# Splitting a weight load to start the first FFN products on four banks, with packed query transposes and re-placed exponentials and loads

## Chip, cores, metric

The kernel runs on one core of one Trainium2 chip. The metric is the device time of a whole execution in microseconds (us). The profile is one execution, with times from the start of the core's span. A load has *landed* when the trace records the last of its completions. (The prediction and the expectations speak of last packets and of instruction fetches instead, on a clock that reads about 0.24 us more than the timelines shown here: the fetch put at 17.35 us there starts at 17.11 us here.)

## The reference, cut to what matters

```python
# 8 batches, 8 heads, 1024 rows, head size 64, 64 projected rows
k_proj = einsum('ks,bhsd->bhkd', E, k);  v_proj = einsum('ks,bhsd->bhkd', F, v)
attn = softmax(q @ k_proj^T / sqrt(64));  x = attn @ v_proj       # then (8192, 512)
h = maximum(maximum(x @ w1, x @ w2), x @ w3)                       # 512 -> 768
out = h @ w_out                                                    # 768 -> 512
```

## The kernel before

All engines are scheduled by hand: program order is execution order on each engine. Batch by batch, the FFN of one batch runs on TensorE (PE) while the attention of the next is slipped between its products. PE writes into eight PSUM banks. `two()` and `bank()` deal them out at build time by an estimated clock.

At the start, the loads are queued in the order of need. The first FFN products, half-batch 0 of batch 0, take six banks and begin once the first two quarters of w1 are there:

```python
    load_w(0, slice(0, 2))          # w1, quarters 0 and 1
    load_kv(2, V2); load_kv(2, V3)  # v of head pairs 2 and 3
    load_w(0, slice(2, 3)) ...
    # before the first product, while waiting for w1:
    v_pair(1); idle(1); x(1); z(2); z(3); at(18.2)

    def up_first(work):             # (cut) products of w1, quarter by quarter
        h = [... for t, ns in (two(), two(), two()) for n in (0, 1)]
        for ct in range(NCT):
            for jt in jts:
                up_mm(h[jt][0], 0, 0, 0, jt, (ct,))
                then((0, ct, jt))   # attention pieces hung behind a product
```

`v_pair(g)` projects v of head pair g (PE, then a VectorE copy), `z(g)` are the softmax sums, `x(g)` the values times the inverse sums. `qp` turns q of the second half-batch on PE, `sc` are scores (PE) with their exp (ScalarE), `za` sums, inverse and values together. `plan(b)` says behind which FFN step of batch b each piece of batch b+1 runs:

```python
        if b == 0: ...
                (1, 2): [vproj(1), ld(2)],
                (1, (3, "mid")): [sc(1, 0), sc(1, 1)],
                (1, 4): [za(1, 0), sc(1, 2)],
        if b == 1: ...
                (0, 3): [kproj(2), vproj(2), ld(3, (0, 1))],     # q and k of batch 3
                (0, 8): [zc(2, nc.gpsimd), ld(3, (2,))],         # broadcasts; v of batch 3
```

`zc(2)` computes batch 2's inverse sums compactly, writes them to DRAM (`zd`) and broadcasts them back into `zi_all` by four DMAs.

The softmax here doesn't subtract the row's maximum and nothing guards it: scores larger than these inputs give would overflow.

## Time and profile before

| reading | value | view |
|---|---|---|
| time, median of 3 | 403.15 us (403.04 to 403.41) | timing |
| span, PE busy, granted clock | 401.0 us, 97%, 1.00 | the page |
| chain that ended last | 80% PE, 11% DMA | the page |
| PE waits that matter | 1.3 us for w1; 0.3 for batch 1's v; 0.7 for hT | waits |

From the page, the busy times and the shares of the chain that ended last, kernel before:

```profile
PE 388.7 (97%) x2261; PEld 176.7 (44%) x2303; DVE 203.3 (51%) x319; ACT 149.0 (37%) x238; POOL 34.1 (9%) x48
PE 80%; DMA 11%; DVE 3%; issue 2%; ACT 2%; POOL 1%; DVEq 0%; ACTq 0%; POOLq 0%
```

The waits of PE in the kernel before (who waited for whom: total us, times, longest):

```profile
PE banks L567 <- DMA w_sb<-in_moe_w_dram: 1.3, 1, 1.3
...
PE banks L664 <- DVE hT L577: 0.7, 1, 0.7
PE banks L470 <- DMA k_t<-in_k_dram: 0.6, 1, 0.6
...
PE banks L345 <- DMA v_t<-in_v_dram: 0.3, 1, 0.3
```

PE is full, so time can only be gained by taking away its waits (5.5 us in all in the list of waits, without 1.6 us that end in "issue", for which the trace names no cause) or its work. The timeline says where these waits are. A line is: start, duration, engine, source line, operation, output<-input, count, and in brackets the idle time before it and what ended that.

PE in the kernel before, timeline:

```profile
16.63 0.62 PE L496 MATMUL banks<-v_t,efT 128*128 128x128 bf16 x8
17.08 0.38 PE L441 MATMUL banks<-warm 128*128 128x512 bf16 x1
...
19.44 1.24 PE L567 MATMUL banks<-xT,w_sb 128*128 128x512 bf16 x5 [1.29 <-DMA w_sb<-in_moe_w_dram]
...
38.75 0.48 PE L211 MATMUL banks<-qT,kpT 64*64 64x256 bf16 x4
...
55.95 1.06 PE L345 MATMUL banks<-v_t,efT 128*64 128x256 bf16 x16 [0.32 <-DMA v_t<-in_v_dram]
...
66.78 0.41 PE L231 MATMUL banks<-pT,ones 64*64 64x512 bf16 x4 [0.35 <-DVE xT L308]
...
67.21 0.57 PE L211 MATMUL banks<-qT,kpT 64*64 64x512 bf16 x4
...
117.83 0.39 PE L664 MATMUL banks<-wout_sb,hT 128*128 128x512 bf16 x1 [0.70 <-DVE hT L577]
```

The line at 16.63 is `v_pair(1)`; its start will be the mark from which stretches are counted. The wait at 117.83 begins with a DMA: the broadcasts of batch 2's inverse sums are issued late, and VectorE's scaling waits for them. GpSimd in the kernel before, timeline:

```profile
104.81 2.58 POOL L275 DMA_DIRECT2D zi_all<-zd  x4 [15.42 <-DMA zd<-zic]
```

VectorE in the kernel before, timeline:

```profile
112.63 2.35 DVE L308 TENSOR_TENSOR xT<-banks,zi_all 128x1024 bf16<-128x1024 f32 x2 [1.70 <-PE banks L567]
```

The bracket names PE, but PE's values were done at 110.8 us. The trace records the second broadcast as landed at 112.50 us, just before the scaling starts: that is the wait. The broadcasts were late because the store of `zd`, issued at 99.76 us, landed only at 104.27, at nearly the same time as batch 3's k (104.52), which was queued before it.

### The profile page before, as it was taken

To read this page: it belongs to the slowest core of one execution; us is meant where nothing else is said; L and a number is where in the kernel's file an instruction comes from. 1 tells how busy PE (TensorE), PEld (TensorE's weight loads), DVE (VectorE), ACT (ScalarE), POOL (GpSimd) and SP (SyncE) were. 2 spreads that over 40 slices of the span, in tenths; PEclk is the share of its full clock that TensorE was granted. 3 is DMA by queue.
4 is the path that set the end of the run, shared out by engine and by line. 5 is a ranking of instruction groups with operands and counts; after the bars stand their busy time and mean duration, and the time that the engine had idled before them with its cause. 6 is when DMAs were issued, how large, how long until landed. Compare 5 with 4: busy or idle time off the path is not lost.

```text
span 401.0 us, 5737 instructions
## 1 busy us (share of the span) xinstructions
PE 388.7 (97%) x2261; PEld 176.7 (44%) x2303; DVE 203.3 (51%) x319; ACT 149.0 (37%) x238; POOL 34.1 (9%) x48
## 2 busy tenths in 40 slices
PE   7899999999999999999999999999999999999996
PEld 3444444353435435444454445444454444444443
DVE  3348755761673525826274544744267342745251
ACT  2622537527213452253323542245323533132312
POOL 7340002010301000200020000200000000000000
PEclk9999999999999999999999999999999999999999
DMA  9999999969799989999899959992890229020202
GB/s 157 206 205 207 231 202 156 240 137 187 222 183 253 191 171 209 174 227 181 205 222 180 236 122 217 211 235 63 203 217 2 105 65 252 3 106 0 105 2 105
DMA packets 66315, 66.11 MB, mean 165 GB/s; under 512 B 30608, under 2 KB 58768, under 8 KB 66288
## 3 DMA queue, kind: packets, MB, share of 16 engines
q0 software_dynamic: 29088, 30.41, 47.2%
q1 hardware_dynamic: 37056, 35.20, 34.9%
q8 instruction: 18, 0.29, 0.3%
q10 hardware_dynamic: 144, 0.13, 0.1%
q14 instruction: 9, 0.07, 0.1%
HBM read 69.73 MB, written 16.97 MB: 216 GB/s over the span
## 4 chain that ended last, share of the span: by engine, by line
PE 80%; DMA 11%; DVE 3%; issue 2%; ACT 2%; POOL 1%; DVEq 0%; ACTq 0%; POOLq 0%
PE banks L567 54%; PE banks L664 18%; DMA v_t<-in_v_dram 8%; DMA w_sb<-in_moe_w_dram 3%; PE banks L345 3%; PE banks L231 2%; DVE xT L308 2%; PE banks L211 2%; PE banks L256 1%; ACT zi_all L297 1%; ACT zl L291 1%; DVE m L629 1%; DVE hT L577 0%; POOL k_t L152 0%; POOL q_t L157 0%
## 5 line engine op out<-in xcount | busy, mean ns | idle before, releaser
L567 PE MATMUL banks<-xT,w_sb 128*128 128x512 bf16 x1119 | 254.8, 379 | 3.8 <-DMA w_sb<-in_moe_w_dram 1.3
L567 PEld LDWEIGHTS <-w_sb 128*128 128x128 bf16 x1152 | 110.0, 98 | 137.5 <-issue 8.7
L629 DVE TENSOR_TENSOR m<-banks,h1s 128x512 f32<-128x512 f32 x90 | 62.1, 690 | 135.7 <-ACT h1s L625 92.4
L625 ACT COPY h1s<-banks 128x512 f32<-128x512 f32 x90 | 52.6, 585 | 119.7 <-PE banks L567 119.6
L664 PE MATMUL banks<-wout_sb,hT 128*128 128x512 bf16 x370 | 85.8, 379 | 1.7 <-issue 0.8
L577 DVE TENSOR_TENSOR hT<-banks,m 128x512 bf16<-128x512 f32 x90 | 62.3, 692 | 10.4 <-PE banks L567 0.8
L664 PEld LDWEIGHTS <-hT 128*128 128x128 bf16 x378 | 35.3, 98 | 48.8 <-issue 5.8
L102 ACT COPY o_sb<-banks 128x512 f32<-128x512 f32 (+1 forms) x56 | 32.6, 582 | 58.7 <-PE banks L664 58.3
L222 ACT ACTIVATE pT<-banks 128x1024 bf16<-128x1024 f32 (+1 forms) x36 | 32.7, 932 | 25.3 <-PE banks L211 25.3
L308 DVE TENSOR_TENSOR xT<-banks,zi_all 128x1024 bf16<-128x1024 f32 x28 | 33.2, 1220 | 12.0 <-PE banks L231 5.5
L200 POOL DMA_DIRECT2D q_t<-in_q_dram x7 | 6.1, 877 | 192.9 <-DMA qT<-q_p 102.4
L102 DVE CAST vp<-banks 64x256 bf16<-64x256 f32 (+1 forms) x18 | 7.1, 397 | 12.4 <-ACT vp L102 8.8
L345 PEld LDWEIGHTS <-efT 128*64 128x64 bf16 x224 | 11.6, 110 | 3.8 <-issue 3.0
L102 ACT CAST vp<-banks 64x256 bf16<-64x256 f32 x14 | 5.1, 364 | 20.7 <-PE banks L345 20.6
L231 PE MATMUL banks<-pT,vp 64*64 64x512 bf16 (+1 forms) x144 | 11.4, 363 | 0.4 <-DVE vp L102 0.4
L211 PE MATMUL banks<-qT,kpT 64*64 64x512 bf16 (+1 forms) x144 | 11.2, 361 | 0.0
L291 ACT ACTIVATE zl<-banks 128x512 f32<-128x512 f32 (+1 forms) x12 | 8.9, 739 | 5.2 <-PE banks L231 4.4
L102 DVE COPY q_p<-q_t 128x1024 bf16<-128x1024 bf16 x28 | 10.1, 425 | 0.0
L102 DVE COPY o_sb<-banks 128x512 f32<-128x512 f32 (+1 forms) x9 | 5.8, 654 | 4.5 <-PE banks L644 4.5
L441 PE MATMUL banks<-warm_f 128*128 128x512 f32 x8 | 6.6, 977 | 1.5 <-DVE warm_f L175 1.5
L345 PE MATMUL banks<-v_t,efT 128*64 128x256 bf16 x112 | 7.3, 273 | 0.3 <-DMA v_t<-in_v_dram 0.3
L345 PE MATMUL banks<-k_t,efT 128*64 128x256 bf16 x112 | 7.5, 276 | 0.0
(60 smaller groups left out, 119.0 us busy)
## 6 DMA issues: line engine op xcount, KB each, us to landing
out_dram<-o_sb SPq DMA_DIRECT2D x30, 512.0 KB, 5.0
zi_all<-zd SPq DMA_DIRECT2D x20, 512.0 KB, 7.9
q_t<-in_q_dram POOLq DMA_DIRECT2D x7, 1024.0 KB, 9.5
k_t<-in_k_dram POOLq DMA_DIRECT2D x7, 1024.0 KB, 16.0
v_t<-in_v_dram POOLq DMA_DIRECT2D x7, 1024.0 KB, 21.1
zi_all<-zd POOLq DMA_DIRECT2D x4, 512.0 KB, 8.0
w_sb<-in_moe_w_dram POOLq DMA_DIRECT2D x5, 384.0 KB, 12.6
k_t<-in_k_dram POOLq DMA_DIRECT2D x2, 512.0 KB, 8.8
```

Source lines behind the costliest of these rows:

```text
L102: done = {"v": nc.vector.tensor_copy, "s": nc.scalar.copy, "g": nc.gpsimd.tensor_copy}[eng](out=o, in_=i)
L211: nc.tensor.matmul(out=t[c * HALF:(c + 1) * HALF, hp, 0:n * P], lhsT=kpTs[b][rows, g, :], rhs=qTs[b][rows, at:at + n, :], start=True, stop ...
L222: nc.scalar.activation(out=pTs[b, g, lo], in_=t, func=AF.Exp, scale=scale)
L231: nc.tensor.matmul(out=t[hp * HALF:(hp + 1) * HALF, c, 0:nsi * HALF], lhsT=w(rows, hp), rhs=p[rows, hp, :], start=True, stop=True,)
L291: nc.scalar.activation(out=zl, in_=t, func=AF.Ln)
L308: nc.vector.tensor_tensor(out=xTs[b][:, g, lo:lo + nsi, :].rearrange("a (c s) p -> a c (s p)", c=2), in0=t, in1=zi, op=ALU.mult,)
L345: nc.tensor.matmul(out=t[hh * HALF:(hh + 1) * HALF, 0:width], lhsT=efT[:, si, (kv - 1) * KP:kv * KP], rhs=qkv[b][kv][:, heads[hh], si, :], ...
L567: nc.tensor.matmul(out=h, lhsT=w_sb[i][:, ct, jt * P:(jt + 1) * P], rhs=xTs[b][:, ct, ch * SPC:(ch + 1) * SPC, :], start=(ct == first), st ...
L577: nc.vector.tensor_tensor(out=o, in0=h, in1=other, op=ALU.max)
L625: nc.scalar.copy(out=h1s, in_=h[0][0])
L629: nc.vector.tensor_tensor(out=m12, in0=h[1][0], in1=h1s, op=ALU.max)
L664: nc.tensor.matmul(out=o_ps, lhsT=hTs[b, ch][:, jt, tt * P:(tt + 1) * P], rhs=wout_sb[:, jt, :], start=(jt == 0), stop=(jt == NJT - 1),)
```

## The change

The intent is to start the first FFN products as soon as one quarter of w1 is there, on four banks, with the rest of the attention start between them; to turn the second half of q as full-width packed transposes; and to re-place some exps and loads of the later schedule. The diff, cut:

```diff
-    load_w(0, slice(0, 2))
+    load_w(0, slice(0, 1))
+    load_w(0, slice(1, 2))
...
+    def pack_q(b, gs, lo, nsi):        # VectorE copies two heads side by side
...
     def qp(b, gs, lo, nsi):
-                heads_q(b, g, range(lo, lo + nsi), t[:, i * n:(i + 1) * n])
+                for si in range(nsi):
+                    nc.tensor.transpose(... in_=q_pk[b][:, g, lo + si] ..., identity=ident)
...
     v_pair(1)
-    idle(1)
-    x(1)
-    z(2)
-    z(3)
-    at(18.2)
+    at(17.4)
...
-        for ct in range(NCT):
-            for jt in jts:
+        for ct, js in (
+            (0, range(0, 4)), (1, range(0, 4)), (0, range(4, 6)), (1, range(4, 6)),
+            (2, jts), (3, jts),
+        ):
+            for jt in js:               # banks taken two at a time, when first needed
...
-                (1, (3, "mid")): [sc(1, 0), sc(1, 1)],
-                (1, 4): [za(1, 0), sc(1, 2)],
+                (1, (3, "mid")): [sc(1, 0, now=True), sc(1, 1)],
+                (1, 4): [za(1, 0), sc(1, 2, now=True)],
...
-                (0, 3): [kproj(2), vproj(2), ld(3, (0, 1))],
+                (0, 3): [kproj(2), vproj(2), ld(3, (0,))],
-                (0, 8): [zc(2, nc.gpsimd), ld(3, (2,))],
+                (0, 8): [zc(2, nc.gpsimd), ld(3, (1, 2))],
...
-                (1, 6): [vx(3, 2), vx(3, 3), sc(4, 0)],
+                (1, 7): [vx(3, 2), vx(3, 3), sc(4, 0)],
...
+                    (0, 0, 1): [lambda: x(1)],
+                    (0, 0, 3): [lambda: z(2), lambda: z(3)],
+                    (0, 1, 3): [lambda: v_pair(2), lambda: x(2)],
...
-                    (2, "a", 2): [qp(0, (0, 1), *c1)],
-                    (2, "a", 4): [qp(0, (2, 3), *c1)],
-                    (2, 0): [sc(0, 0, *c1)],
-                    (2, 2): [sc(0, 1, *c1)],
+                    (2, "a", 0): [pack_q(0, (0, 1), *c1)],
+                    (2, "a", 1): [pack_q(0, (2, 3), *c1)],
+                    (2, "a", 4): [qp(0, (0, 1), *c1)],
+                    (2, "a", 5): [qp(0, (2, 3), *c1)],
+                    (2, 1): [sc(0, 0, *c1)],
+                    (2, 3): [sc(0, 1, *c1)],
```

More of the change, by code (lines that the diff above doesn't have):

```diff
@@ L361, in heads_q, with qp, f @@
         pe(0.08 * len(sis))
-    def qp(b, gs, lo=0, nsi=SI):
+    q_pk = {}
+    def pack_q(b, gs, lo, nsi):
         def f():
-            if b not in qTs:
-                qTs[b] = att.tile([P, NPAIR * SI, P], BF16, name="qT")
+            if b not in q_pk:
+                q_pk[b] = att.tile([P, NPAIR, SI, 2, D], BF16, name="q_p", bufs=1)
+            for g in gs:
+                copy(
+                    "v", q_pk[b][:, g, lo:lo + nsi].rearrange("p si h d -> p h si d"),
+                    qkv[b][0][:, 2 * g:2 * g + 2, lo:lo + nsi], (), 0.25,
+                )
+        return f
+    def qp(b, gs, lo, nsi):
+        def f():
             t, ns = two()
@@ L370, in f @@
             for i, g in enumerate(gs):
-                heads_q(b, g, range(lo, lo + nsi), t[:, i * n:(i + 1) * n])
+                for si in range(nsi):
+                    nc.tensor.transpose(
+                        out=t[:, i * n + si * P:i * n + (si + 1) * P],
+                        in_=q_pk[b][:, g, lo + si].rearrange("p h d -> p (h d)"),
+                        identity=ident,
+                    )
+                pe(0.06 * nsi)
             o = qTs[b].rearrange("a (g si) p -> a g si p", si=SI)
@@ L590, in up_first @@
         jts = range(NJT)
-        h = [(t[:, n], ns[n:n + 1]) for t, ns in (two(), two(), two()) for n in (0, 1)]
-        for ct in range(NCT):
-            for jt in jts:
+        h = {}
+        for ct, js in (
[3 more added lines that the diff above has]
+            for jt in js:
+                if jt not in h:
+                    t, ns = two()
+                    for n in (0, 1):
+                        h[jt + n] = t[:, n], ns[n:n + 1]
                 up_mm(h[jt][0], 0, 0, 0, jt, (ct,))
@@ L753 @@
                 up_first({
-                    (0, 0, 5): [lambda: v_pair(2)],
-                    (0, 1, 2): [lambda: x(2)],
+                    (0, 0, 1): [lambda: x(1)],
+                    (0, 0, 3): [lambda: z(2), lambda: z(3)],
+                    (0, 1, 3): [lambda: v_pair(2), lambda: x(2)],
                     (0, 1, 5): [lambda: v_pair(3), ld(1)],
-                    (0, 2, 2): [lambda: x(3)],
-                    (2, "a", 2): [qp(0, (0, 1), *c1)],
-                    (2, "a", 4): [qp(0, (2, 3), *c1)],
-                    (2, 0): [sc(0, 0, *c1)],
-                    (2, 2): [sc(0, 1, *c1)],
+                    (0, 2, 1): [lambda: x(3)],
+                    (2, "a", 0): [pack_q(0, (0, 1), *c1)],
[4 more added lines that the diff above has]
+                    (2, 3): [sc(0, 1, *c1)],
                     (2, 4): [za(0, 0, *c1, then=True), sc(0, 2, *c1)],
```

## The prediction

> **What bounds the kernel now.** TensorE: the page shows PE busy 97% of 401.0 us at a granted clock of 1.00, and 80% of the chain of waits is PE. Three of its waits matter. (a) Until 19.2 us for w1's first part (1.3 us; first product at 19.44). (b) At 55.5 us the value projection of batch 1 waits for v (PE 0.3, weight loads 0.8 us); the DMA engines are full from 3 to 59 us, and v's last packet ends at 55.9. (c) At 117.8 us a down product waits 0.70 us for hT.
>
> **What the change does.**
> 1. *Split of w1's first part, start on four banks.* Half of it should land 0.95 us earlier (the whole took 1.9 us per DMA engine), and gains more: the packet records show one engine about 1 us late because a 16,384-byte instruction fetch sat on it from 17.35 to 18.33 us (the Trainium skill, "Runtime: NRT & Kernel Launch", Instruction fetch mechanics, says streams are refilled in 16 KiB blocks by DMA; this trace agrees, 18 such packets). The first half should pass before the fetch: landed at 17.4, first product at 17.6 us, 1.8 us earlier. The second half still lands near 19.2. But x(1) and the sums of pairs 2 and 3 (0.7 us on PE, done before while waiting) now follow the start, and x(2) directly follows its v_pair, a stall of about 0.5 us (copy 0.29 plus handovers). Net at the first pass's last part (25.16 before): 0.4 to 0.8 us earlier.
> 2. *Packed q.* 32 half-width transposes (0.64 us per 16) become 16 full-width (0.77 for 8 in the E/F turn): no gain on PE. Four more DVE copies, about 0.25 us each (1024 wide took 0.42), behind maxima that end at 33.4: up to 0.3 us of stall.
> 3. *Then PE meets (b).* Batch 1's v is limited by the bytes queued since the start: near 55.9 us again; the wait grows by what the start won. So 1 and 2 count as about 0.
> 4. *Exps of batch 1 at once:* may remove waits at 66.4 and 76.3 us (0.35 and 0.16), may add bank waits: 0.1 gained.
> 5. *k of batch 3 later, behind the zi broadcasts.* Before, k's load ran to 104.4 us, the zi issue waited until 104.8, and DVE's first batch-2 scaling stood until 112.6 (1.7 us idle) for the broadcast; the maxima behind it made (c). Now the broadcasts start about 2 us earlier and (c) should go: 0.7 gained. The price: v of batch 3 comes near 127.5 to 128.5 instead of 124.2, and is wanted at about 128: 0.2 lost on average, perhaps 1.
> 6. *Batch 2, step (1,7):* 0 to 0.2 gained.
>
> **Sum:** -0.7: **402.5 us, range 401.4 to 403.5.** Faster by over 2%: 0.01; within 2%: 0.98; slower: 0.01.
>
> **What would show it.** Timeline: first FFN product near 17.6, last part of the first pass near 24.6, PE's wait for batch 1's v 0.8 to 1.3 us, that projection at 55.6 to 56.3 as before. PE waits: no 0.7 us on hT near 117; DVE's first batch-2 scaling near 111. A PE wait on v near 127 would show step 5's price.
>
> **What would make it wrong.** If batch 1's v lands earlier too, the start's 0.5 us stays: 402.0 or less. If the packed copies or the changed bank order stall PE by a microsecond, or batch 3's v is over 1 us late: equal or worse.

## The result, and the profile after

The changed kernel takes 403.22 us (median of 4, 402.96 to 403.75), the kernel before 403.10 in the same rounds. The ratio is 1.0005, 95% interval 0.9987 to 1.0022: the same. (A ratio here is the mean time of one kernel's fast runs over that of the other's in the same rounds, so not quite the ratio of the quoted medians.) All outputs are right. In a second call it was 402.40 against 402.78, ratio 0.9988 (0.9966 to 1.0009): again the same.

From the page, kernel after:

```profile
PE 392.7 (98%) x2286; PEld 176.6 (44%) x2286; DVE 204.1 (51%) x323; ACT 149.0 (37%) x238; POOL 34.4 (9%) x49
PE 84%; DMA 8%; DVE 3%; ACT 2%; issue 2%; POOL 1%; DVEq 0%; POOLq 0%; ACTq 0%
```

PE's busy time rose by 4.0 us in a span of equal length. This is not more work: the profile before lacks records, showing 1119 products with w_sb where it has 1152 weight loads for them, and the one after shows all 1152. The changed kernel profiled once more (e11) shows 1119 again, and 387.8 us busy. The Trainium skill, "Trainium Kernel Development and Optimization", Performance Expectations, calls matmul busy time a bad metric for how close a kernel is to roofline, because matmuls are pipelined. Busy time misleads, but for another reason, missing records; no run here tests the reason that the skill gives.

The waits of PE, kernel after:

```profile
PE banks L346 <- DMA v_t<-in_v_dram: 0.7, 1, 0.7
PE banks L232 <- DVE vp L102: 0.7, 2, 0.5
PE banks L212 <- ACT zl L292: 0.5, 1, 0.5
PE banks L490 <- DMA k_t<-in_k_dram: 0.5, 1, 0.5
PE banks L386 <- DVE qT L102: 0.3, 1, 0.3
...
PE banks L212 <- DVE m L652: 0.3, 1, 0.3
```

Both aims were reached: the waits for w1 and for hT are gone. In their place stand waits for copies, for a logarithm of ScalarE, for a maximum of VectorE, and for a v. PE, kernel after, timeline:

```profile
16.53 0.62 PE L516 MATMUL banks<-v_t,efT 128*128 128x128 bf16 x8
17.32 0.59 PE L583 MATMUL banks<-xT,w_sb 128*128 128x512 bf16 x2 [0.17 <-DVE xT L309]
...
34.66 0.61 PE L386 MATMUL banks<-ident,q_p 128*128 128x128 bf16 x8 [0.35 <-DVE qT L102]
...
39.08 0.30 PE L212 MATMUL banks<-qT,kpT 64*64 64x256 bf16 x4 [0.52 <-ACT zl L292]
...
55.72 1.06 PE L346 MATMUL banks<-v_t,efT 128*64 128x256 bf16 x16
...
66.20 0.41 PE L232 MATMUL banks<-pT,ones 64*64 64x512 bf16 x4
...
66.76 0.37 PE L212 MATMUL banks<-qT,kpT 64*64 64x512 bf16 x1
67.40 0.41 PE L212 MATMUL banks<-qT,kpT 64*64 64x512 bf16 x3 [0.27 <-DVE m L652]
...
128.80 1.06 PE L346 MATMUL banks<-v_t,efT 128*64 128x256 bf16 x16 [0.71 <-DMA v_t<-in_v_dram]
```

The first product comes at 17.32 instead of 19.44 us. The score at 39.08 is the one that stood at 38.75 before without a wait. The line at 128.80 is batch 3's value projection and says 0.71; that v belongs to batch 3, not to batch 1. GpSimd and then VectorE, kernel after, timeline (the second a fence of its own):

```profile
102.18 2.38 POOL L276 DMA_DIRECT2D zi_all<-zd  x4 [12.86 <-DMA zd<-zic]
```

```profile
110.89 2.35 DVE L309 TENSOR_TENSOR xT<-banks,zi_all 128x1024 bf16<-128x1024 f32 x2
```

The store of `zd`, issued at 99.80 us, now landed at 101.61, the broadcasts went out 2.6 us earlier, and VectorE's scaling followed its own work without a wait.

To see who gave and who took, I cut PE's timeline at points that all versions have, and take differences of start times. The **mark** is the start of `v_pair(1)`. A mark is needed because the first loads do not land at the same time in each execution: over the 14 profiles (kernel before, changed kernel, 12 experiments) the first key projection started between 9.58 and 10.92 us, whatever the kernel. That spread alone is larger than most effects below. It also makes repeated runs scatter: 11 runs of the kernel before went from 401.85 to 404.91.

| stretch on PE, us | before | after | after, second profile |
|---|---|---|---|
| mark to first FFN product | 2.81 | 0.79 | 0.78 |
| A: mark to FFN of half-batch 1 | 29.85 | 30.11 | 29.99 |
| B: to batch 1's value projection | 9.47 | 9.08 | 9.07 |
| C: to batch 2's key projection | 29.05 | 29.32 | 29.31 |
| D: to batch 3's key projection | 42.87 | 41.99 | 41.99 |
| E: to batch 3's value projection | 0.90 | 1.77 | 0.90 |
| F: to the last down products | 267.44 | 267.47 | 267.44 |
| mark to last, sum of A to F | 379.58 | 379.74 | 378.70 |

The start is 2.0 us earlier (first row), and nothing of it is left at the end of A. About three quarters is gone within the first pass of products, as foreseen: its last part starts at 24.64 us, against 25.16 before, since `x(1)`, `z(2)` and `z(3)`, which ran inside the wait for w1 before, now follow the start, and PE waits 0.45 us for the copy behind `v_pair(2)`. The last half microsecond is what e5 and e7 look for. C loses 0.27, D gains 0.88, and E took 0.87 back in the first profile and nothing in the second. Two thirds of the run, F, did not notice anything.

### The profile page after: what moved, and what is told of

Same layout as the page of the kernel before. It is cut to its first block, busy times and chain, and to the rows that moved or that the text cites. A ratio compares the mean times of both kernels' runs of the same rounds, so it can differ in the third digit from the quotient of the medians.

```text
span 401.0 us, 5752 instructions
## 1 busy us (share of the span) xinstructions
PE 392.7 (98%) x2286; PEld 176.6 (44%) x2286; DVE 204.1 (51%) x323; ACT 149.0 (37%) x238; POOL 34.4 (9%) x49
## 4 chain that ended last, share of the span: by engine, by line
PE 84%; DMA 8%; DVE 3%; ACT 2%; issue 2%; POOL 1%; DVEq 0%; POOLq 0%; ACTq 0%
PE banks L583 55%; PE banks L687 18%; DMA v_t<-in_v_dram 6%; PE banks L346 3%; PE banks L232 2%; PE banks L212 2%; DMA k_t<-in_k_dram 2%; DVE xT L309 1%; PE banks L257 1%; ACT zl L292 1%; DVE hT L593 1%; ACT zi_all L298 1%; PE banks L490 1%; DVE m L652 0%; PE banks L461 0%
## 5 line engine op out<-in xcount | busy, mean ns | idle before, releaser
L583 PE MATMUL banks<-xT,w_sb 128*128 128x512 bf16 x1152 | 257.6, 379 | 0.3 <-DVE xT L309 0.3
L687 PE MATMUL banks<-wout_sb,hT 128*128 128x512 bf16 x378 | 86.9, 380 | 0.1
L102 DVE COPY q_p<-q_t 128x1024 bf16<-128x1024 bf16 (+1 forms) x32 | 11.3, 417 | 0.0
```

What stands on the lines that cost most here:

```text
L102: done = {"v": nc.vector.tensor_copy, "s": nc.scalar.copy, "g": nc.gpsimd.tensor_copy}[eng](out=o, in_=i)
L583: nc.tensor.matmul(out=h, lhsT=w_sb[i][:, ct, jt * P:(jt + 1) * P], rhs=xTs[b][:, ct, ch * SPC:(ch + 1) * SPC, :], start=(ct == first), st ...
L687: nc.tensor.matmul(out=o_ps, lhsT=hTs[b, ch][:, jt, tt * P:(tt + 1) * P], rhs=wout_sb[:, jt, :], start=(jt == 0), stop=(jt == NJT - 1),)
```

## Experiments

Theory: leads are swallowed one by one by waits whose end does not depend on PE's lead, either DMAs or another engine's queue. Rivals: the later schedule loses what the start gains; the packed turns cost the lead; the exps and not the load order took the hT wait away. Every run was timed in 5 rounds beside the kernel before.

| run | median, us | before, us | ratio to before (95%) |
|---|---|---|---|
| e1_start_only | 403.66 | 402.58 | 1.0017 (1.0000 to 1.0034) |
| e2_plan_only | 402.09 | 402.58 | 0.9981 (0.9965 to 0.9996) |
| e3_k_half_early | 402.62 | 402.58 | 0.9993 (0.9978 to 1.0007) |
| e4_one_w1_part | 403.81 | 402.58 | 1.0034 (1.0007 to 1.0060) |
| e5_score_later | 402.57 | 402.76 | 0.9992 (0.9976 to 1.0008) |
| e6_score_later_k_half | 402.66 | 402.76 | 0.9993 (0.9979 to 1.0007) |
| e7_old_q_turn | 402.40 | 402.76 | 0.9990 (0.9977 to 1.0004) |
| e8_old_load_order | 403.50 | 402.76 | 1.0014 (0.9999 to 1.0029) |
| e9_best | 402.18 | 402.78 | 0.9980 (0.9960 to 1.0001) |
| e10_best_v_later | 401.56 | 402.78 | 0.9966 (0.9944 to 0.9988) |
| e11_changed_again | 402.40 | 402.78 | 0.9988 (0.9966 to 1.0009) |
| e12_old_start | 401.47 | 403.25 | 0.9956 (0.9943 to 0.9970) |

The stretches of the same runs, in the letters of the table above:

| run | first product | A | B | C | D | E |
|---|---|---|---|---|---|---|
| e1_start_only | 0.79 | 29.99 | 9.27 | 29.05 | 42.88 | 0.90 |
| e2_plan_only | 2.94 | 29.98 | 9.36 | 29.31 | 41.99 | 0.90 |
| e3_k_half_early | 0.79 | 29.99 | 9.07 | 29.31 | 41.99 | 0.90 |
| e4_one_w1_part | 1.42 | 30.64 | 9.07 | 29.31 | 42.00 | 0.90 |
| e5_score_later | 0.79 | 29.56 | 9.51 | 29.31 | 42.00 | 0.89 |
| e6_score_later_k_half | 0.78 | 29.81 | 9.10 | 29.31 | 42.00 | 0.89 |
| e7_old_q_turn | 0.78 | 29.29 | 9.33 | 29.31 | 42.00 | 0.89 |
| e8_old_load_order | 0.79 | 29.99 | 9.19 | 29.31 | 42.48 | 0.90 |
| e9_best | 0.78 | 29.35 | 10.36 | 29.05 | 42.00 | 0.89 |
| e10_best_v_later | 0.79 | 29.32 | B+C 38.74 | | 42.00 | 0.90 |
| e12_old_start | 1.46 | 29.42 | B+C 38.14 | | 41.99 | 0.90 |

Where B+C is given, batch 1's value projection was moved; before, B+C is 38.52. F was 267.43 to 267.47 in all of them. C and D repeat to 0.01 us among profiles of the same code, so they are a far finer ruler than the times. A is less good: e5 and e6, with the same code there, differ by 0.25 us, because in e6 the v of pair 2 landed later. B depends on when the loads of that execution came: over the 14 profiles batch 1's v landed between 55.10 and 56.57 us, while the mark moved from 16.48 to 17.81 us, and the two do not move together. An execution with a late mark therefore waits less in B, and its end counted from the mark looks better than it is.

### One half of the change each: e1 and e2

e1 is the changed kernel with the `plan` of before; e2 is the kernel before with the `plan` of the changed one.

```diff
 e1 (against the changed kernel), e2 the other way round (against the kernel before)
-                (1, (3, "mid")): [sc(1, 0, now=True), sc(1, 1)],
-                (1, 4): [za(1, 0), sc(1, 2, now=True)],
+                (1, (3, "mid")): [sc(1, 0), sc(1, 1)],
+                (1, 4): [za(1, 0), sc(1, 2)],
-                (0, 3): [... ld(3, (0,))],      (0, 8): [... ld(3, (1, 2))],
+                (0, 3): [... ld(3, (0, 1))],    (0, 8): [... ld(3, (2,))],
-                (1, 7): [vx(3, 2), vx(3, 3), sc(4, 0)],
+                (1, 6): [vx(3, 2), vx(3, 3), sc(4, 0)],
```

> Only the start of the change (split of w1's first part, four banks, packed q); the later schedule as before. Theory (leads are swallowed one by one): first FFN product near 17.3 us and about 0.5 us of lead over before at 38 us, but the first product of the second half-batch at 46.5 to 46.8 us as before and batch 1's value projection at 55.6 to 56.0; the 0.7 us wait on hT near 117 us is back; no wait for batch 3's v; total within 0.2 us of before (403.2). Rival (the start is worth something and the later schedule loses it again): 0.4 us or more faster than before.

Measured: first product 0.79 us after the mark, A 29.99, so no lead is left at half-batch 1. The hT wait is back. PE in e1, timeline:

```profile
118.37 0.39 PE L687 MATMUL banks<-wout_sb,hT 128*128 128x512 bf16 x1 [0.71 <-DVE hT L593]
```

The time was not "within 0.2": it is 0.17% (0.7 us) above before with an interval that just touches 1. This profile's first key projection came 0.6 us later than that of the kernel before, while its stretches add up to 379.53, against 379.58. The start alone therefore gains nothing; whether it costs something in time is not settled by these runs.

> Only the later schedule of the change (exps at once, k of batch 3 behind the broadcasts, step 1,7); the start as before. Theory: no wait on hT near 117 us, 0.7 to 0.9 us ahead of before at 122 us, then a wait of 0.6 to 0.8 us for batch 3's v near 128 us that takes all of it back; total within 0.2 us of before. Rival (it is the earlier start that took the hT wait away): the hT wait stays, and the v wait with it or not, total up to 0.7 us slower than before.

Measured: no hT wait, D 41.99, which is 0.88 us better than before. The wait for batch 3's v was expected at 0.6 to 0.8 us and did not come: v landed at 128.05 us and PE came at 128.10. C shows a loss of 0.26 us that I had not expected. Together 0.19% (0.8 us) faster than before, so "within 0.2" was missed here too. The plan without the start does at least as well as the whole change: its interval overlaps those of the changed kernel (0.9987 to 1.0022, and 0.9966 to 1.0009), so that it is better is not shown. The hT wait goes without any lead from the start, against the rival.

### What the exps at once cost: C in all runs

C is 29.05 us in the three profiles that keep the old place of batch 1's exps (before, e1, e9) and 29.31 or 29.32 in the nine that issue them at once and leave the value projection in its place. The `now=True` costs 0.26 us. The mechanism is in ScalarE's order: an exp now stands before the copy `h1s` of an FFN step. ScalarE in the kernel before, timeline:

```profile
65.37 0.57 ACT L625 COPY h1s<-banks 128x512 f32<-128x512 f32 x1
65.83 1.03 ACT L222 ACTIVATE pT<-banks 128x1024 bf16<-128x1024 f32 x1
```

ScalarE in the kernel after, timeline:

```profile
65.14 1.01 ACT L223 ACTIVATE pT<-banks 128x1024 bf16<-128x1024 f32 x1
66.05 0.58 ACT L648 COPY h1s<-banks 128x512 f32<-128x512 f32 x1
```

VectorE's maximum needs `h1s`, and the bank that the maximum frees is the one that the next score was dealt: it is the wait of 0.27 us at 67.40 in the PE timeline after. The exps at once did remove the wait of 0.35 us at 66.78, as intended, but then 0.64 us lie between the first and the second product of the score (66.76 and 67.40), against 0.17 before; that takes back more than was won.

### Load order: e8, and e3

e8 puts only the load order back. The diff is the second pair of lines of the one above.

> The changed kernel with batch 3's k loaded with its q as before, v alone behind the broadcasts. Theory (the broadcasts waited behind k): zi issue at 104.5 us or later, VectorE's first batch-2 scaling at 112 or later, the hT wait of 0.6 to 0.8 us near 117 us back, no wait for batch 3's v; end within 0.3 us of the changed kernel. Rival (the exps at once or the step 1,7 took the hT wait away): no hT wait and no v wait, end 0.7 us earlier than the changed kernel.

GpSimd in e8, then VectorE in e8, timeline:

```profile
105.27 2.57 POOL L276 DMA_DIRECT2D zi_all<-zd  x4 [15.37 <-DMA zd<-zic]
```

```profile
112.75 2.36 DVE L309 TENSOR_TENSOR xT<-banks,zi_all 128x1024 bf16<-128x1024 f32 x2 [1.30 <-DMA zi_all<-zd]
```

The broadcasts are late again and here the trace names them as what VectorE waited for. The hT wait is back at 0.3 us, not the 0.6 to 0.8 expected, and D is 42.48: about half of the 0.88 us is lost again. `zd`, issued at 100.28 us, landed at 104.72, and k at 104.38. That the load order is what matters is shown. The size of the wait is not explained by when PE came: in e1, which has the old load order too, PE came equally late (key projection of batch 2 at 85.53 us there, 85.51 here) and waited 0.71 us. The difference is in the broadcasts: the second landed at 112.62 us here and at 113.05 in e1, issued only 0.15 us earlier. Why it was quicker here stays open. The time of this profiled execution is no measure of the load order either: it ends 6.2 us after the start of its last down products, against 4.7 to 4.8 in all other profiles, for a reason that the profile does not name.

e3 is the changed kernel with k of batch 3 loaded in halves.

```diff
 (cut: load() and ld() take the heads to load)
-                (0, 3): [kproj(2), vproj(2), ld(3, (0,))],
-                (0, 8): [zc(2, nc.gpsimd), ld(3, (1, 2))],
+                (0, 3): [kproj(2), vproj(2), ld(3, (0,)), ld(3, (1,), LO)],
+                (0, 8): [zc(2, nc.gpsimd), ld(3, (1,), HI), ld(3, (2,))],
```

> The changed kernel with the first half of batch 3's k loaded right behind its q, where the queues ran dry (97 to 102 us), the other half and v behind the broadcasts. Theory: the broadcasts are issued within 0.5 us of 102.2 as in the changed kernel, v's last packet 2.0 to 2.6 us earlier than 128.65 us, no wait for it on PE, the 0.8 us gained at 117 us stays to the end: 402.4 us, 0.6 to 0.9 us faster than the changed kernel. Rival (k's half delays the broadcasts as the whole k did before): broadcasts issued after 104 us, hT wait back, total unchanged.

Measured: v landed at 126.53 us, 2.2 earlier than in the changed kernel; no wait for it; D kept at 41.99; mark to last 378.70. The broadcasts went out at 103.79, later than the expected bound, and here the rival is partly right: the half of k landed at 102.21 us and `zd`, issued at 100.45, only at 103.25. In the other runs with halves (e6, e9, e10, e12) that half landed at 99.80 to 100.81 and `zd` at 101.81 to 102.41. The delay stayed too small to bring the hT wait back. The time, 402.62, did not show the gain: the changed kernel itself, run again (e11), had no wait in E either.

> The changed kernel once more, in the rounds of its repairs. Theory: same to 0.3 us as before in time; second half-batch at 30.0 to 30.1 after the mark, 29.31 us from batch 1's value projection to batch 2's key projection. Batch 3's v was waited for in one profile of the changed kernel (0.71 us) and in none of four variants with the same loads there: its last packet came 110.4 to 112.1 us after the mark and is wanted at about 111.5, so here a wait of 0 to 0.9 us; end 378.9 to 379.8.

Measured: E 0.90, no wait; v landed at 128.21 us, just in time for PE at 128.32. So the wait of 0.71 us in the first profile is one outcome among several: of the five profiles in which the loads of batch 3's k and v stand as in the changed kernel and q is packed or not (e2, e4, e5, e7, e11), none waited. Loading half of k early takes the risk away (v landed at 124.35 to 126.53 us in e3, e6, e9, e10, e12). It does not, by itself, show in the time.

### The start: e4, e5, e7

e4 joins w1's first part again and leaves all else as changed.

> The changed kernel with w1's first part in one load again, all else as changed: the start comes about 2 us later. Theory (waits further on have slack): first FFN product near 19.4 us, lag of 1.5 to 2 us at 30 us, about 0.5 us at batch 1's value projection (56.2 instead of 55.7), nothing left after batch 3's v wait (128.8, the wait shrinks by the lag); total 0 to 0.5 us slower than the changed kernel. Rival (PE-bound from the start on): 1.5 to 2 us slower, 405.

PE in e4, timeline:

```profile
18.72 0.60 PE L582 MATMUL banks<-xT,w_sb 128*128 128x512 bf16 x2 [0.81 <-DMA w_sb<-in_moe_w_dram]
```

The start came only 0.63 us later than with the split (1.42 against 0.79 after the mark), not 2; A became 0.65 longer than in the second profile of the changed kernel. Up to the end of A, a delay of the start thus passes on in full in this code. The end is 379.35 after the mark, 0.65 more than in e11, so it passes on to the end as well: the theory, by which nothing was to be left of it, failed here. Two of its six timed runs (405.01 and 406.07) ran at a mean granted clock of 0.994 and 0.992, so its ratio overstates the loss.

Why 0.63 and not 2? The mark is a large part of it. In the kernel before, e2, e4 and e12 the joined part landed at 19.17, 19.23, 18.68 and 19.21 us, and the mark stood at 16.63, 16.56, 17.30 and 17.81. In e4 the load landed 0.49 us earlier than before and PE came 0.67 us later; in e12 the load was no earlier, PE only came 1.18 us later to it. A late execution thus hides the wait for w1. The prediction gave a 16,384-byte instruction fetch as what held up the last DMA engine. In the kernel before it lasts from 17.11 to 18.09 us; 15 of the 16 completions of the load are recorded by 18.07 and the last at 19.17. But in e12 the fetch begins only at 18.33 and the last completion still comes 1.1 us after the other 15 (18.09 and 19.21). The records do not name the engine of a packet; that the fetch delayed the load in the kernel before is argued, and it is not the only thing that makes one engine late.

e5 moves one score by two products, so that ScalarE has freed its banks.

```diff
-                    (2, 4): [za(0, 0, *c1, then=True), sc(0, 2, *c1)],
+                    (2, 4): [za(0, 0, *c1, then=True)],
+                    (2, 5): [sc(0, 2, *c1)],
```

> The changed kernel with the third score of the second half-batch two products later, so that its banks are free when PE comes to it. All times from the start of the value projection of pair 1, since the first loads land up to 0.8 us earlier or later from run to run. Theory (the start's lead dies at the 0.52 us wait of that score for ScalarE's logarithm): that wait falls to 0.15 us or less, first product of the second half-batch 29.6 to 29.75 us after the mark (before 29.85, changed 30.11). Then the lead is eaten by later waits, batch 1's v, batch 1's softmax, at the latest batch 3's v (wait 0.7 to 1.2 us): end 379.4 to 379.8 after the mark (before 379.58, changed 379.74), total within 0.3 us of the changed kernel. Rival (nothing is lost further on): end 379.2 or less.

Measured: A 29.56, as expected (29.99 in e11), so this one wait was worth 0.43 us. I had expected a later wait to take it; B did take some (a wait of 0.36 us for batch 1's v, B 9.51), but no wait for batch 3's v came, and the end was 378.71, the rival's range. In time it is not clear of before (0.9992).

e7 is the changed kernel with the old, half-width turns of q at their old places.

```diff
-                    (2, "a", 0): [pack_q(0, (0, 1), *c1)],   ... (2, "a", 4) and (2, "a", 5): [qp(...)]
+                    (2, "a", 2): [qp(0, (0, 1), *c1)],
+                    (2, "a", 4): [qp(0, (2, 3), *c1)],       # and the scores back to (2, 0), (2, 2)
```

> The changed kernel with the old half-width turns of q at their old places. Theory: the score's banks are again freed by VectorE and its 0.52 us wait is gone, lead of 0.3 to 0.6 us over before at the first product of the second half-batch (29.25 to 29.55 us after the mark, before 29.85). With 32 more PE instruction pairs the third 16 KB instruction fetch comes near 51 us again, before batch 1's v is through, and v's last packet 0.4 to 0.9 us later than in the changed kernel (55.6 to 56.0); PE waits there 0.8 us or more and the lead is gone: value projection of batch 1 at 39.1 to 39.4 after the mark; total within 0.3 us of the changed kernel. Rival (packed q is what costs the lead, and without it the gain stays): end 379.2 or less after the mark.

PE in e7, timeline:

```profile
34.55 0.64 PE L357 MATMUL banks<-ident,q_t 128*64 128x128 bf16 x16
...
38.73 0.48 PE L212 MATMUL banks<-qT,kpT 64*64 64x256 bf16 x4
...
55.80 1.06 PE L346 MATMUL banks<-v_t,efT 128*64 128x256 bf16 x16 [0.19 <-DMA v_t<-in_v_dram]
```

Neither the turn nor the score waits. A is 29.29: the start's lead of 0.56 us over before is there, and the packed turns had cost 0.7 (29.99 to 29.29). The two forms take PE alike (0.64 us for 16 half-width turns, 0.61 for 8 full-width). The cost is the 0.35 us wait for the copy out and, above all, the other deal of banks: the score at 38.73 here, like that at 38.75 before, is released by a semaphore of VectorE, that at 39.08 after by one of ScalarE, and e5 gave 0.43 of the 0.7 us to this score's wait. My expectation that this lead would be gone at batch 1's value projection was not met in this run: its execution began late (mark 17.18), and batch 1's v, which landed at 55.76, made PE wait only 0.19. The rival is right that the packed turns cost the lead; the end, 378.27 after the mark, is in its range, helped by the late mark. In time, 0.9990, it is not clear of before.

### Both repairs together: e6

> Both repairs: score later, and half of batch 3's k early. Theory: as with half of k early alone (end 378.70 after the mark of pair 1's value projection) or up to 0.4 us better, as the start's lead may pass batch 1's softmax or not; no wait for batch 3's v; total 0.8 to 1.3 us faster than the changed kernel in the same rounds and 0.6 to 1.2 us faster than before.

Measured: no wait for v, last products at 378.55 after the mark, within what was expected; the time, 402.66 against 402.76 of before, is not the expected 0.6 to 1.2 us faster. The runs of this kernel went from 402.00 to 403.40. A gain of under 0.3% needs more runs than these to be seen in the time.

### The wait that takes the start: e9, e10, e12

e9 keeps what gained (the start, the later k, now in halves) and puts back what cost (turns and exps as before).

> Only the parts that the earlier runs showed to gain: w1's split with the four-bank start, the old turns of q, the old places of batch 1's exps, k of batch 3 half with its q and half behind the broadcasts. Theory (each part is worth what its own stretch showed): second half-batch 29.3 us after the mark of pair 1's value projection, batch 1's value projection at 38.4 to 39.3 (not before 55.7 us of absolute time), from there to batch 2's key projection 29.05 instead of 29.31, then 42.0, no wait for batch 3's v; end 377.8 to 378.7 after the mark, 0.9 to 1.8 us less than before, total 1.0 to 1.6 us faster than before in the same rounds. Rival (a gain in one stretch comes back as a wait in the next): end 379.2 or later.

PE in e9, timeline:

```profile
56.19 1.06 PE L348 MATMUL banks<-v_t,efT 128*64 128x256 bf16 x16 [1.22 <-DMA v_t<-in_v_dram]
```

A is 29.35: PE comes to batch 1's value projection with its lead, in an execution whose first loads came early (mark 16.48), and waits 1.22 us there. B is 10.36, the lead is spent. This is what the prediction had said of the changed kernel. The wait is 0.90 us longer than before; 0.5 of it is the start's lead (A), 0.15 the earlier mark, and 0.24 a later v, which landed at 56.14 us, against 55.90 before and 55.19 and 55.94 in the two profiles of the changed kernel: a DMA that does not heed how early PE started. The mark to last is 379.10, above the expected 377.8 to 378.7; the time, 0.9980, is at the edge of clear and short of the expected 1.0 to 1.6 us.

e10 then moves that projection one FFN step later.

```diff
-                (1, 2): [vproj(1), ld(2)],
+                (1, 3): [vproj(1), ld(2)],
```

> The same with batch 1's value projection one step (2.7 us) later, so that its v is there whenever PE comes. Theory (that v is the only barrier between 30 and 60 us): no wait on v, second half-batch to batch 2's key projection 0 to 0.9 us shorter than in the run without this; end 377.4 to 377.9 after the mark. Rival (batch 2's v is now loaded too late, or the softmax of batch 1 waits for its values instead): a new wait near 63 or 86 us that takes it back.

PE in e10, timeline:

```profile
57.88 0.63 PE L214 MATMUL banks<-qT,kpT 64*64 64x512 bf16 x8 [0.55 <-DMA qT<-q_p]
```

No wait for v, and 401.56 us, 0.34% faster than before. But the next DMA is right behind: the scores of batch 1 wait 0.55 us for the transposed q, which moves through the same DMA engines. The end after the mark, 378.40, missed the expected 377.4 to 377.9 by that.

e12 asks whether the early start is worth anything now. It is the kernel before with the halved k, the later value projection and the step (1,7), nothing else.

> The fastest version so far (score exps and q turns as before, k of batch 3 in halves, batch 1's value projection a step later), but with the start of the kernel before: w1's first part in one load, six banks, first FFN product when all of it is there. Theory (with its later barriers moved, the early start is worth what it leads by at the second half-batch, 0.5 us): first product 2.8 us after the mark, second half-batch at 29.85 to 30.0 (29.32 with the early start), no v wait, end 378.7 to 379.0 after the mark (378.40 with the early start), 0.4 to 0.9 us faster than before in the same rounds. Rival (the start is worth nothing even then): end 378.3 to 378.5.

PE in e12, timeline:

```profile
19.27 1.74 PE L569 MATMUL banks<-xT,w_sb 128*128 128x512 bf16 x6
...
58.03 0.63 PE L213 MATMUL banks<-qT,kpT 64*64 64x512 bf16 x8
```

It takes 401.47 us, 0.44% faster than before, and is the fastest version along with e10, which has the early start. The expected cost of the old start did not show: this execution began late (mark 17.81), PE came to w1 when it was almost there (first product 1.46 after the mark, not 2.8), and at the scores of batch 1 it stands at 58.03 us without a wait where e10 stands at 57.88 after one. The end, 377.89 after the mark, is below both the expected 378.7 to 379.0 and the rival's 378.3 to 378.5, so this late profile tests neither well. I expected the start to be worth 0.5 us even here; by the times, the rival, that it is worth nothing, fits better. e10 and e12 were timed in different rounds, so that they are equal is only as good as two overlapping intervals.

## Why the prediction was right or wrong

The time, 402.5 us with 401.4 to 403.5, held the measured 403.22 (and 402.40 in the second). "The same within 2%" was right. The range is 2.1 us wide, more than twice what any one stretch from A to E gained or lost against before, so that it held says little about the steps, and they were not all right.

1. *Start.* Right. Landed for a first product at 17.32 us (17.6 predicted), 2.1 us earlier than before; the first pass's last part came at 24.64 as predicted (the fifth product of the block that starts at 23.70), 0.52 us earlier than before (0.4 to 0.8 predicted).
2. *Packed q.* The step that failed most in size: "up to 0.3 us of stall". It cost 0.7 us (A 29.99 against 29.29 in e7). The 0.35 us wait for the copy I had; the 0.52 us wait of a score for ScalarE's logarithm I had not, because I costed instructions and did not look at which bank the score would be dealt.
3. *Batch 1's v.* The sum "1 and 2 count as about 0" held, for the wrong reason in this kernel: the lead was gone at 39 us, and PE did not wait for that v in the changed kernel. The mechanism is real: once the packed turns were out (e9), the wait was 1.22 us, inside the predicted 0.8 to 1.3, and B took the lead. That size is partly luck: 0.15 us came from an early execution and 0.24 from a later v, and e7, in a late execution, waited only 0.19.
4. *Exps at once.* Wrong in sign: 0.1 us gained was predicted, 0.26 lost was measured. The wait at 66.4 went, as foreseen, and the bank waits that I called possible were larger (0.64 us between two products of a score, against 0.17 before).
5. *k of batch 3 later.* Right in mechanism, and near in size: 0.88 us gained (0.7 predicted), the scaling at 110.9 (111 predicted), a wait for v near 128 in one profile (0.71 us, at the top of "perhaps 1"), none in the second or in the four variants with the same load order and no halved k.
6. *Step (1,7).* Nothing: F is 267.44 with and without it.

The sum of -0.7 us became +0.16 in the stretches of the first profile, because of step 4 (C +0.27) and of v's wait (E +0.87, where 0.2 on average had been counted); D gave more than foreseen (-0.88). Step 2's cost did not enter the sum, since A and B together were counted as nothing and came to -0.13. In the second profile, without the wait in E, the stretches sum to -0.88. So whether the sum holds depends on an execution's wait for batch 3's v, and that is luck here. The two timings, 1.0005 and 0.9988, do not separate these cases.

The Trainium skill, "DMA: Bandwidth & Descriptors", Issuing engines are not separate DMA queues, says that DMAs from the SP, ACT and GpSimd queues share the same 16 engines and interleave. The traces agree, and it is the likely reason why step 3's v is late: before, batch 1's q and k take about 5.1 us each from first to last packet (packets counted off in order, since they do not name their load), and its v, in whose time an output write and the transposes of q run, takes 9.7: from 50 to 51 us, for example, 153 packets of the load and 153 of the transposes start. No run took those transfers away.

## What to carry to other kernels

An earlier start is worth only what passes the next wait that does not move with it: before building one, list the following DMA arrivals and other engines' chains in order of time, and look at how much slack each has. When banks are dealt at build time, a moved instruction can wait for another engine; look at who frees the bank, not only at what the instruction costs. Compare stretches between fixed points of the trace when run-to-run scatter (here 3 us over 11 runs) is larger than the effect, and check first whether a stretch contains a wait for a DMA: then a late execution shortens it (e12).

## What the Trainium skill lacked or had wrong

- "Runtime: NRT & Kernel Launch", Instruction fetch mechanics, calls the cost of crossing a 16 KiB boundary mostly hidden. It says nothing of the data loads in flight. The profile before shows 18 packets of 16,384 bytes that take 0.88 to 1.53 us each, and the one after has one of 2.77 us. Whether they hold up loads stays open: the load in flight at the first of them completed 1.1 us later on one engine than on the other 15, but so did the same load in e12, where the fetch came later (18.33 us).
- No page that I read says how much the landing of the first loads varies from execution to execution: the first key projection, which waits for the second of them, started from 9.58 to 10.92 us over 14 profiles, whatever the kernel.
- "DMA: Bandwidth & Descriptors" says that queues interleave, but gives no figure for what a load loses beside a DMA transpose and a write: here about 9.7 us instead of 5.1 for 1 MB.
